# Second buffers for the loads of q and k in an attention and FFN kernel, loads issued a pair earlier, and a new table of times for its scheduler

## The chip, the cores and the metric

One core of a Trainium2 chip runs the whole program. The metric is the time of one execution on the device in microseconds (us). The engines are TensorE (PE; its weight loads are PEld), VectorE (DVE), ScalarE (ACT), GpSimd (POOL) and SyncE (SP), which in this kernel issues every DMA, in order, from one queue.

## The reference

Attention with pairs of queries averaged, then a feed-forward layer whose gate is a cosine. Everything is float32; q and k are drawn eight times larger than v.

```python
# q, k, v: (8 batches, 8 heads, 1152, 64)
q_pool = q.reshape(B, H, S // 2, 2, D).mean(axis=3)          # 576 queries
scores = (1 / sqrt(D)) * matmul(q_pool, k.transpose(0, 1, 3, 2))
scores = scores - max(scores, axis=-1)
attn = exp(scores); attn = attn / (sum(attn, axis=-1) + 1e-09)
x = matmul(attn, v)              # to (8 * 576, 512): heads side by side
h = x @ w_in                     # 512 x 2048
out = (h * cos(h)) @ w_out       # 2048 x 512
```

## The kernel before

**Precision.** Each float32 operand is split in two float16 parts, high and low, and a product is made of two or three float16 matmuls.

**Pairs and units.** The work is cut into 32 pairs (two heads of one batch), pair `n`. A pair has ten units: unit 0 takes the 64 remaining queries of each head, units 1 to 9 take one block of 128 keys each against 512 queries of both heads. A unit makes scores on PE (tile `st`, L880, and L900 for unit 0), the exponential on ACT (`e`, L926), the float16 high part on ACT (`pp`, L929), the low part on POOL or DVE (`pp`, L935 and L931; for unit 0's short rest `pps`), and one unit later the products with v on PE (`ava`, `avb`, L950). The first four pairs (`NDIR`) run the products with v in float32 and without the split (L921).

**What is prepared for a pair ahead of it.** This is what the change touches, step by step:

- k comes in two pieces, J0 (4 of the 9 blocks) and J1 (5). `load_k` loads a piece into `kld` (L576), `prep_k` splits it into `kst` (ACT L604, POOL L605), `transpose_k` transposes it by DMA into one of three `k1` (L650), `copy_k` copies that to one of two `k2` (L657).
- `load_q` loads q into `qld` by four DMAs (two of 256 KB at L586, two of 32 KB at L593). `pool_q` adds the two queries of a pair in place (POOL L611). `prep_q1` writes the high part into `q1s` (L622 on ACT in the first four pairs, then L624 on DVE), and `transpose_q1` transposes that into one of three `q1T` (L629). `prep_q2` writes the low part into `qs2` (POOL L637, L643).
- The row maxima: `mains` and the `mx_` steps multiply q1T with k on PE (`mx`, L675, L693, L715, L732), and DVE reduces each result to maxima (`mxs`, L685, L703, L725, L742), which frees the bank for PE's next one. `m_write` puts the maxima into `qs2`, and `transpose_q2` transposes it into one of two `q2T` (L764).
- `load_v` loads v into its one buffer `vld` (L770), `v_max_begin` reduces its absolute maximum (DVE L777), writes it to DRAM as `row` (512 bytes, L398) and reads it back spread over all partitions as `am` (L400), `v_max_end` reduces that (L405), `prep_v` and `prep_v_lo` split v (ACT L801, DVE L810).

`qld`, `kld`, `kst` and `qs2` have one buffer each, so a load can only be issued when the pair before is done with the tile.

**The FFN** runs beside the attention as a stream of pieces: xT by DMA transposes (L1115), first matmuls (`f`, L1195), evacuation and cosine (L1217 to L1221, L1144, L1150), the split of the gate (`g`, ACT L1159, POOL L1160), second matmuls (L1251) and output (L1267, L1273). The FFN weights are loaded and split during the first pairs. What is left of the FFN after the last pair is the tail.

**What sets the order.** The program is first written down in one order: at each unit of the running pair `p`, the entries `(dp, di, step)` of `JOBS` with `di` equal to the unit run `step(p - dp)`; so `(-2, 1, pool_q)` prepares pair `p + 2` at unit 1 of pair `p`. Then `arrange` lays every engine's instructions anew: it goes through the program in an estimated time, with a cost for each instruction (`estimate`, `transfer`), a delay between engines (`SEM`), and the buffers' limits (`BUFS`); whenever an engine is free it takes, of its instructions whose inputs are ready in that estimate, the one that was written first. The result is fixed in the program: on the chip each engine runs its list in order.

```python
    JOBS = [
        (-2, 0, lambda n: load_k(n, J0)),
        (-2, 0, load_q),
        (-2, 1, lambda n: prep_k(n, J0)),
        (-2, 1, pool_q),
        ...
```

Of the kernel before, what the change touches and what calls it, by code (L numbers as in the profile page):

```python
# [9 lines left out]
F32 = mybir.dt.float32  # L10
# [42 lines left out]
    "e": NE, "pp": NPP, "q1T": 3, "q2T": 2, "xp": NXP, "xT": NXT, "g": NG, "f": 2,  # L53
    "vam": 4, "es": 1, "pps": 1, "amx": 4,
}
POOL_BUFS = {"sb1": 1, "sb2": 2, "psum": 1, "dram": 1}
SIZES = {"float32": 4, "uint32": 4, "int32": 4, "float16": 2}
SEM = 0.10
BOOST = {}
FILL_LATE = 0  # L60
COLD = 0

# [25 lines left out]
def estimate(ins, kind, rd, wr):  # L88


    eng = str(ins.engine).split(".")[-1]
    n = max([a[2] for a in rd + wr] or [1])
    psum = any(str(a[0].space).endswith("PSUM") for a in rd)
    big = sum(a[2] > 1 for a in rd)
    if eng == "PE":
        return max(n_out(wr) * 0.000421, 0.027), False
    if eng == "Pool":
        return 0.08 + 0.00205 * n, True
    if eng == "Activation":
        return 0.19 + 0.0009 * n, False  # L100
    if kind == "InstTensorReduce":
        return 0.1 + 0.00109 * n, False
    if kind == "InstTensorTensor" or (kind == "InstTensorScalarPtr" and big > 1):
        return 0.14 + 0.00112 * n, not psum
# [26 lines left out]
def arrange(tc, nc, extra, fill):  # L131
# [3 lines left out]
    for i in rec:  # L135
        rd, wr = boxes(i)
        eng = str(i.engine).split(".")[-1]
        if eng == "PE":
# [7 lines left out]
            size = tuple(i.tile_size)  # L146
            c = max(n_out(wr) * 0.000421, 0.027)
            if COLD and i.name in fill:
                c = 0.112
            if rd[0][4] == 4:  # L150
                c = max(n_out(wr) * 0.00345, 0.112)
            if size[0] == 64 and tuple(i.tile_position)[0] == 64:
                c = 0.0
            nd["cost"] += c
            nd["tile"] = size[0]
        else:
            nd = dict(eng=eng, ins=[], rd=[], wr=[], cost=0.0, lock=False)
            nodes.append(nd)
            if eng == "SP":
                nd["cost"] = 0.06  # L160
                nd["dma"], nd["lat"] = transfer(type(i).__name__, rd[0], wr[0])
# [156 lines left out]
def tile_attention_ffn(  # L318
# [253 lines left out]
    def load_k(n, js):  # L572
        b, hp = divmod(n, HP)
        nj = js.stop - js.start
        kt = sb1.tile([P, 2, KT - RB, D], F32, tag="kld", name="kld")
        nc.sync.dma_start(  # L576
            kt[:, :, 0:nj],
            k[b, 2 * hp : 2 * hp + 2].rearrange("h (p j) d -> p h j d", p=P)[:, :, js],
        )
        kld[n] = kt[:, :, 0:nj]  # L580

    def load_q(n):
        b, hp = divmod(n, HP)
        qt = sb1.tile([P, NSL, 2, D], F32, tag="qld", name="qld")
        for h in range(2):
# [13 lines left out]
    def prep_k(n, js):  # L599
        kv = kld[n].rearrange("p h j d -> p j h d")  # L600
        nj = js.stop - js.start
        ks = sb1.tile([P, KT - RB, 4, D], F16, tag="kst", name="kst")[:, 0:nj]
        hi = ks[:, :, 0::3, :]
        nc.scalar.copy(hi, kv)  # L604
# [216 lines left out]
    def mains(c, ts):  # L821
# [628 lines left out]
```

## Time and profile before

| what | value |
|---|---|
| median of 3 runs | 1704.35 us (1699.76 to 1707.55) |
| the profiled execution | 1700.43 us, of which the span from first to last instruction is 1698.6 us |
| mean granted TensorE clock | 0.975 of full speed |
| busy share of the span | PE 92%, ACT 72%, DVE 69%, PEld 63%, POOL 53% |
| DMA | 147.36 MB, mean 87 GB/s |

The profile is of one execution. "Idle before <- releaser" says how long an engine stood and what ended it. In a list of waits the three numbers are the total in us, the number of times and the longest. The chain is the work that ended last, followed back from the end. The granted clock is what the throttle allowed TensorE; a busy PE at half clock does half the work.

### The profile page before, as it was taken

What the parts mean: (1) busy time and instruction counts of PE and PEld (TensorE: products, weight loads), DVE (VectorE), ACT (ScalarE), POOL (GpSimd) and SP (SyncE); (2) the same over time, 40 slices, a digit from 0 to 9 for tenths busy, and PEclk for the clock granted to TensorE, in tenths of its full rate; (3) what the DMA queues carried; (4) which work ended last, traced back from release to release, by engine and by line L of the source; (5) the groups of instructions that cost most, each with busy time, mean ns of one, the idle gap of its engine ahead of it and who ended that gap; (6) DMA issues with size and microseconds to landing.
All of it is one profiled execution on the core that took longest, in us unless ns stands there. A gap on an engine that the chain in (4) does not pass through costs nothing.

```text
span 1698.6 us, 40564 instructions
## 1 busy us (share of the span) xinstructions
PE 1570.6 (92%) x17080; PEld 1070.4 (63%) x17080; DVE 1175.2 (69%) x1686; ACT 1217.3 (72%) x1484; POOL 903.5 (53%) x766
## 2 busy tenths in 40 slices
PE   3898999998999988989999999999999999997998
PEld 1677777664766555655766566666666666665664
DVE  5887887678768767777866677787777777632332
ACT  2445468887887877876987686988688878884442
POOL 3323355567575754656575456666746574461222
PEclk9999999999999999999999999999999999998999
DMA  9976745235535453244534324345424442101000
GB/s 197 197 165 130 153 116 75 64 86 109 95 57 114 84 110 63 66 90 95 97 80 96 75 50 101 80 86 105 100 57 97 81 108 60 27 21 27 13 26 19
DMA packets 340662, 147.36 MB, mean 87 GB/s; under 512 B 247808, under 2 KB 323584, under 8 KB 340480
## 3 DMA queue, kind: packets, MB, share of 16 engines
q1 hardware_dynamic: 340480, 144.78, 41.2%
q8 instruction: 133, 2.18, 0.6%
q14 instruction: 49, 0.40, 0.1%
HBM read 76.55 MB, written 10.50 MB: 51 GB/s over the span
## 4 chain that ended last, share of the span: by engine, by line
PE 69%; DVE 10%; DMA 8%; ACT 6%; issue 3%; POOL 3%; SPq 2%; POOLq 0%; ACTq 0%; DVEq 0%
PE f L1251 20%; PE f L1195 16%; PE st L880 11%; PE ava L950 6%; PE avb L950 5%; PE mx L675 5%; DMA qld<-in_q_dram 4%; DVE mxs L685 2%; DVE q1s L624 2%; ACT e L926 2%; PE avb L1019 2%; PE mx L715 1%; DMA k<-kst 1%; POOL pp L935 1%; DMA xT<-xs 1%
## 5 line engine op out<-in xcount | busy, mean ns | idle before, releaser
L935 POOL TENSOR_TENSOR pp<-e,pp 128x512 f16<-128x512 f32 x374 | 453.2, 1234 | 303.9 <-ACT pp L929 155.2
L1195 PE MATMUL f<-xT,w 128*128 128x256 f16 x3456 | 415.0, 276 | 14.7 <-DVE y L1221 8.6
L685 DVE TENSOR_REDUCE mxs<-mx 128x2 f32<-128x1024 f32 x252 | 307.8, 1221 | 148.1 <-PE mx L675 146.9
L926 ACT ACTIVATE e<-st,eb 128x1024 f32<-128x1024 f32 x280 | 311.1, 1111 | 129.4 <-PE st L880 100.4
L1195 PEld LDWEIGHTS <-w 128*128 128x128 f16 x3456 | 340.7, 99 | 88.8 <-issue 17.9
L1251 PE MATMUL f<-w,g 128*128 128x512 f16 x1728 | 396.4, 380 | 0.0
L929 ACT CAST pp<-e 128x1024 f16<-128x1024 f32 x280 | 292.4, 1044 | 7.7
L950 PEld LDWEIGHTS <-pp 128*128 128x128 f16 (+1 forms) x7392 | 247.4, 100 | 69.0 <-POOL pp L935 14.5
L1251 PEld LDWEIGHTS <-g 128*128 128x128 f16 x1728 | 166.9, 98 | 193.0 <-issue 3.8
L1160 POOL TENSOR_TENSOR g<-hsc,g 128x512 f16<-128x512 f32 x144 | 194.3, 1374 | 148.5 <-ACT g L1159 140.9
L950 PE MATMUL ava<-vc,pp 128*128 128x64 f16 (+4 forms) x4784 | 245.1, 200 | 12.3 <-POOL pp L935 9.2
L880 PE MATMUL st<-q1T,k 128*128 128x512 f16 x576 | 224.0, 389 | 11.1 <-ACT e L926 8.5
L880 PE MATMUL st<-q2T,k 128*128 128x512 f16 x576 | 223.5, 388 | 0.0
L950 PE MATMUL avb<-vc,pp 128*128 128x65 f16 (+1 forms) x3312 | 207.2, 202 | 3.1 <-POOL pp L935 3.0
L675 PE MATMUL mx<-k,q1T 128*128 128x512 f16 x504 | 157.3, 395 | 25.3 <-DVE mxs L685 9.4
L1221 DVE SCALAR_TENSOR_TENSOR y<-f,r1a,y 128x512 f32<-128x512 f32 x144 | 107.1, 746 | 95.2 <-ACT y L1220 93.1
L880 PEld LDWEIGHTS <-k 128*128 128x128 f16 x1152 | 103.0, 100 | 101.4 <-issue 21.9
L931 DVE TENSOR_TENSOR pp<-e,pp 128x1024 f16<-128x1024 f32 x93 | 134.0, 1440 | 35.1 <-ACT pp L929 34.0
L1217 ACT ACTIVATE hsc<-f,r 128x512 f32<-128x512 f32 x144 | 98.4, 683 | 80.3 <-PE f L1195 80.1
L1150 DVE TENSOR_TENSOR hsc<-hsc,y 128x512 f32<-128x512 f32 x144 | 129.6, 950 | 36.6 <-ACT y L1144 36.2
L605 POOL TENSOR_TENSOR kst<-kld,kst 128x512 f16<-128x512 f32 x64 | 88.9, 1389 | 98.3 <-ACT kst L604 83.7
L675 PEld LDWEIGHTS <-q1T 128*128 128x128 f16 x512 | 47.9, 102 | 92.9 <-issue 36.0
(118 smaller groups left out, 1717.6 us busy)
## 6 DMA issues: line engine op xcount, KB each, us to landing
vld<-in_v_dram SPq DMA_DIRECT2D x32, 576.0 KB, 4.3
qld<-in_q_dram SPq DMA_DIRECT2D x64, 256.0 KB, 4.4
kld<-in_k_dram SPq DMA_DIRECT2D x32, 320.0 KB, 3.8
kld<-in_k_dram SPq DMA_DIRECT2D x32, 256.0 KB, 3.2
wraw<-in_moe_w_in_dram SPq DMA_DIRECT2D x8, 1024.0 KB
wraw<-in_moe_w_out_dram SPq DMA_DIRECT2D x8, 1024.0 KB, 6.0
out_dram<-ob SPq DMA_DIRECT2D x32, 256.0 KB, 2.7
k<-k SPq DMA_DIRECT2D x64, 80.0 KB, 3.1
```

What stands on the lines that cost most here:

```text
L675: nc.tensor.matmul(m[:, h, :], q1T[n][:, 2 * t + h, :], k1[n % 3][:, c * RB : (c + 1) * RB, h, :], start=True, stop=True, skip_group_check ...
L685: nc.vector.reduce_max(mxs[n][:, 2 * t : 2 * t + 2, c], m, axis=AX.X)
L880: nc.tensor.matmul(s[:, h, :].rearrange("p (t c) -> p t c", c=P), w[:, j, h, :], x[:, h : 2 * QT : 2, :], start=part == 0, stop=part == 1, ...
L926: nc.scalar.activation(e, s, AF.Exp, scale=exp_scale, bias=eb)
L929: nc.scalar.copy(pp[:, 0], e)
L931: nc.vector.tensor_sub(pp[:, 1], e, pp[:, 0])
L935: nc.gpsimd.tensor_sub(pp[:, 1, c], e[:, c], pp[:, 0, c])
L950: mm = nc.tensor.matmul(out, w, x, start=start, stop=False, skip_group_check=True)
L1150: nc.vector.tensor_mul(hj, hj, y[:, j : j + 2])
L1160: nc.gpsimd.tensor_sub(gt[:, 1], hj, gt[:, 0])
L1195: mm = nc.tensor.matmul(ps[:, fi, :], w1[wt][:, hp, fs], ck.xT[hp][:, xi, cs], start=n == 0, stop=n == 3 * HP - 1, skip_group_check=True,)
L1251: nc.tensor.matmul(po, gt[:, gi, f % 2, ts_], w2[wt][:, f, :], start=f == 0 and (gi, wt) == (0, 0), stop=f == NF - 1 and (gi, wt) == (1, 0),)
```

## The change

1. `qld`, `kld` and `kst` get two buffers each, and there are two `qs2` (by the parity of the pair); the dictionaries of k pieces are keyed by pair and piece.
2. The loads of k and q move from the unit of their use in pair `p` for `p + 2` to units 5, 6 and 9 for `p + 3`. At the start, three pairs' loads are written ahead of the first unit instead of two.
3. `load_v` moves from unit 8 for `p + 2` to unit 0 for `p + 1`, the steps after it by one unit.
4. The table of times: the delay between engines becomes 0.21 after PE, 0.08 after ACT and 0.06 after the others, instead of 0.10 for all; an issue on SP costs 0.55 (a transpose 1.35) instead of 0.06; POOL, ACT, DVE and PE costs are set anew, and a half-width matmul counts half.

```diff
 BUFS = {
     "e": NE, "pp": NPP, "q1T": 3, "q2T": 2, "xp": NXP, "xT": NXT, "g": NG, "f": 2,
-    "vam": 4, "es": 1, "pps": 1, "amx": 4,
+    "vam": 4, "qld": 2, "kld": 2, "kst": 2, "es": 1, "pps": 1, "amx": 4,
 }
-SEM = 0.10
+HAND = {"PE": 0.21, "Activation": 0.08}
...
     if eng == "Pool":
-        return 0.08 + 0.00205 * n, True
+        return 0.16 + 0.00206 * n, True
     if eng == "Activation":
-        return 0.19 + 0.0009 * n, False
+        return 0.21 + 0.00088 * n, False
...
-            c = max(n_out(wr) * 0.000421, 0.027)
+            c = max(n_out(wr) * 0.0004167 + 0.0025, 0.0295)
...
-                nd["cost"] = 0.06
+                nd["cost"] = 1.35 if "Transpose" in type(i).__name__ else 0.55
...
-        fin = end + SEM
+        fin = end + HAND.get(e, 0.06)
...
-    qs2 = fix.tile([P, NSL, P], F16, name="qs2")
-    nc.gpsimd.memset(qs2, 0.0)
+    qs2s = [fix.tile([P, NSL, P], F16, name=f"qs2_{i}") for i in range(2)]
+    for t in qs2s:
+        nc.gpsimd.memset(t, 0.0)
...
-        kt = sb1.tile([P, 2, KT - RB, D], F32, tag="kld", name="kld")
+        kt = sb1.tile([P, 2, KT - RB, D], F32, tag="kld", bufs=2, name="kld")
...
-        qt = sb1.tile([P, NSL, 2, D], F32, tag="qld", name="qld")
+        qt = sb1.tile([P, NSL, 2, D], F32, tag="qld", bufs=2, name="qld")
...
-        ks = sb1.tile([P, KT - RB, 4, D], F16, tag="kst", name="kst")[:, 0:nj]
+        ks = sb1.tile([P, KT - RB, 4, D], F16, tag="kst", bufs=2, name="kst")[:, 0:nj]
...
     JOBS = [
-        (-2, 0, lambda n: load_k(n, J0)),
-        (-2, 0, load_q),
+        (-3, 5, lambda n: load_k(n, J0)),
+        (-3, 6, load_q),
+        (-3, 9, lambda n: load_k(n, J1)),
         (-2, 1, lambda n: prep_k(n, J0)),
         (-2, 1, pool_q),
         (-2, 1, lambda n: transpose_k(n, J0)),
-        (-2, 2, lambda n: load_k(n, J1)),
         (-2, 2, prep_q1),
...
-        (-2, 8, load_v),
...
-        (-1, 0, v_max_begin),
+        (-1, 0, load_v),
+        (-1, 1, v_max_begin),
...
-        (-1, 4, v_max_end),
-        (-1, 5, prep_v),
-        (-1, 6, lambda n: prep_v_lo(n, (0,))),
-        (-1, 7, lambda n: prep_v_lo(n, (1,))),
+        (-1, 5, v_max_end),
+        (-1, 6, prep_v),
+        (-1, 7, lambda n: prep_v_lo(n, (0,))),
+        (-1, 8, lambda n: prep_v_lo(n, (1,))),
...
-    for n in (0, 1):
+    for n in (0, 1, 2):
```

How the instructions move, for pair 12 as the example. In the rows below a name carries its buffer's number, and the changed kernel's line numbers are mostly one or two off. SP before, from v's load of pair 11 to pair 12's transpose of q1 (`qld_6576` is pair 12's q, `kst_6669` and `kld_6767` its k):

```order
L770 DMA vld_6417<-in_v_dram 128x2x576
L657 DMA k2_1_70<-k1_2_107 64x5x128 x2
L398 DMA row_6589<-mxa_6587 128x1
L586 DMA qld_6576<-in_q_dram 128x4x128
L593 DMA qld_6576<-in_q_dram 64x128 x2
L650 DMA_TRANSPOSE k1_0_105<-kst_6669 128x8x128
L576 DMA kld_6767<-in_k_dram 128x2x320
L586 DMA qld_6576<-in_q_dram 128x4x128
L400 DMA am_6591<-row_6589 128x128
L1073 DMA left_95<-lx_6648 64x64 x2
L629 DMA_TRANSPOSE q1T_6772<-q1s_73 128x10x128
```

The load of q stands right behind `row`, and three rows ahead of the transpose that needs it. SP of the changed kernel, at the load of pair 12's q (`qld_6280`):

```order
L627 DMA_TRANSPOSE q1T_5241<-q1s_75 128x10x128
L396 DMA row_5162<-mxa_5160 128x1
L649 DMA_TRANSPOSE k1_1_108<-kst_5296 128x10x128
L584 DMA qld_6280<-in_q_dram 128x4x128
L591 DMA qld_6280<-in_q_dram 64x128
L1074 DMA left_97<-lx_5136 64x64
L574 DMA kld_6214<-in_k_dram 128x2x256
L591 DMA qld_6280<-in_q_dram 64x128
L584 DMA qld_6280<-in_q_dram 128x4x128
```

It now stands just behind pair 10's transpose of q1 (`q1T_5241`). And 24 rows further on, SP of the changed kernel at pair 12's transpose of q1, from v's load of pair 11 (`vld_6589`):

```order
L771 DMA vld_6589<-in_v_dram 128x2x576
L656 DMA k2_1_70<-k1_2_109 64x5x128 x2
L627 DMA_TRANSPOSE q1T_6774<-q1s_75 128x10x128
L649 DMA_TRANSPOSE k1_0_107<-kst_6842 128x10x128
L396 DMA row_6674<-mxa_6672 128x1
L584 DMA qld_7779<-in_q_dram 128x4x128
L591 DMA qld_7779<-in_q_dram 64x128 x2
L574 DMA kld_7722<-in_k_dram 128x2x256
L584 DMA qld_7779<-in_q_dram 128x4x128
```

The transposes of pair 12 now stand ahead of `row`, and what stands behind `row` are loads for later pairs. POOL before, from pair 12's split of k to its split of q (`pps_6563` is pair 10's):

```order
L605 TENSOR_TENSOR kst_6669<-kld_6574,kst_6669 128x4x128
L935 TENSOR_TENSOR pp_6470<-e_6468,pp_6470 128x512 x2
L935 TENSOR_TENSOR pp_6557<-e_6555,pp_6557 128x512 x2
L935 TENSOR_TENSOR pps_6563<-es_6561,pps_6563 128x128
L611 TENSOR_TENSOR qld_6576<-qld_6576 128x9x64
L935 TENSOR_TENSOR pp_6758<-e_6756,pp_6758 128x512 x2
L605 TENSOR_TENSOR kst_6840<-kld_6767,kst_6840 128x5x128
L935 TENSOR_TENSOR pp_6831<-e_6829,pp_6831 128x512 x2
```

The pooling of q (L611) stands behind pair 10's `pps`, and the `pp` of pair 10 stand behind it. POOL of the changed kernel at the same step of pair 12 (`kst_6667`, `qld_6280`; `pps_5823` is pair 9's, and pair 8's stands six rows ahead of the first row shown):

```order
L603 TENSOR_TENSOR kst_6667<-kld_6214,kst_6667 128x4x128
L609 TENSOR_TENSOR qld_6280<-qld_6280 128x9x64
L636 TENSOR_TENSOR qs2_1_72<-qld_5433,q1s_75 128x4x2x64
L936 TENSOR_TENSOR pp_5554<-e_5552,pp_5554 128x512 x2
L642 TENSOR_TENSOR qs2_1_72<-qld_5433,q1s_75 64x64
L936 TENSOR_TENSOR pp_5628<-e_5626,pp_5628 128x512 x2
L642 TENSOR_TENSOR qs2_1_72<-qld_5433,q1s_75 64x64
L609 TENSOR_TENSOR qld_7036<-qld_7036 128x9x64
L936 TENSOR_TENSOR pp_5817<-e_5815,pp_5817 128x512 x2
L936 TENSOR_TENSOR pps_5823<-es_5821,pps_5823 128x128
```

The pooling of pair 12's q has moved ahead of pair 9's `pps`, and that of pair 13 (`qld_7036`) follows it within the same pair.

More of the change, by code (lines that the diff above doesn't have):

```diff
@@ L57 @@
 SIZES = {"float32": 4, "uint32": 4, "int32": 4, "float16": 2}
-SEM = 0.10
+HAND = {"PE": 0.21, "Activation": 0.08}
 BOOST = {}
 FILL_LATE = 0
-COLD = 0
 def boxes(ins):
@@ L103, in estimate @@
     if kind == "InstTensorTensor" or (kind == "InstTensorScalarPtr" and big > 1):
-        return 0.14 + 0.00112 * n, not psum
+        return 0.15 + 0.00106 * n, not psum
     if kind == "InstTensorScalarPtr":
@@ L146, in arrange @@
             size = tuple(i.tile_size)
-            c = max(n_out(wr) * 0.000421, 0.027)
-            if COLD and i.name in fill:
-                c = 0.112
+            c = max(n_out(wr) * 0.0004167 + 0.0025, 0.0295)
             if rd[0][4] == 4:
-                c = max(n_out(wr) * 0.00345, 0.112)
-            if size[0] == 64 and tuple(i.tile_position)[0] == 64:
-                c = 0.0
+                c = 2 * max(n_out(wr) * 0.00167 + 0.0025, 0.112)
+            if size[1] == 64:
+                c *= 0.5
             nd["cost"] += c
-            nd["tile"] = size[0]
+            nd["tile"] = size
         else:
@@ L249, in arrange @@
     table = None
-    mode = 128
+    mode = (128, 128)
     order = {e: [] for e in engines}
@@ L280, in arrange @@
         if e == "PE" and nd["tile"] != mode:
-            c += 0.1
+            c += 0.15
             mode = nd["tile"]
@@ L579, in load_k @@
         )
-        kld[n] = kt[:, :, 0:nj]
+        kld[n, js.start] = kt[:, :, 0:nj]
     def load_q(n):
         b, hp = divmod(n, HP)
-        qt = sb1.tile([P, NSL, 2, D], F32, tag="qld", name="qld")
+        qt = sb1.tile([P, NSL, 2, D], F32, tag="qld", bufs=2, name="qld")
         for h in range(2):
@@ L599, in prep_k @@
     def prep_k(n, js):
-        kv = kld[n].rearrange("p h j d -> p j h d")
+        kv = kld.pop((n, js.start)).rearrange("p h j d -> p j h d")
         nj = js.stop - js.start
-        ks = sb1.tile([P, KT - RB, 4, D], F16, tag="kst", name="kst")[:, 0:nj]
+        ks = sb1.tile([P, KT - RB, 4, D], F16, tag="kst", bufs=2, name="kst")[:, 0:nj]
         hi = ks[:, :, 0::3, :]
@@ L605, in prep_k @@
         nc.gpsimd.tensor_sub(ks[:, :, 1:3, :], kv, hi)
-        kst[n] = ks
+        kst[n, js.start] = ks
     def pool_q(n):
@@ L634, in prep_q2 @@
     def prep_q2(n):
+        qs2 = qs2s[n % 2]
         qs = qld.pop(n)
@@ L651, in transpose_k @@
             k1[n % 3][:, js].rearrange("p j h c -> p (j h) c"),
-            kst.pop(n).rearrange("p j a d -> p (j a d)"),
+            kst.pop((n, js.start)).rearrange("p j a d -> p (j a d)"),
         )
@@ L744, in m_write @@
     def m_write(n):
+        qs2 = qs2s[n % 2]
         m = sb2.tile([P, NSL], F32, tag="m", name="m")
@@ L762, in transpose_q2 @@
     def transpose_q2(n):
+        qs2 = qs2s[n % 2]
         t = sb1.tile([P, NSL, P], F16, tag="q2T", bufs=2, name="q2T")
```

## The prediction

> **What bounds the kernel now.** I read the page first (engines, then the chain that ended last), then busy time by stretches, then one stall in order of time.
>
> ```profile
> span 1698.6 us, 40564 instructions
> PE 1570.6 (92%) x17080; PEld 1070.4 (63%) x17080; DVE 1175.2 (69%) x1686; ACT 1217.3 (72%) x1484; POOL 903.5 (53%) x766
> ...
> PE 69%; DVE 10%; DMA 8%; ACT 6%; issue 3%; POOL 3%; SPq 2%; POOLq 0%; ACTq 0%; DVEq 0%
> PE f L1251 20%; PE f L1195 16%; PE st L880 11%; PE ava L950 6%; PE avb L950 5%; PE mx L675 5%; DMA qld<-in_q_dram 4%; DVE mxs L685 2%; DVE q1s L624 2%; ACT e L926 2%; PE avb L1019 2%; PE mx L715 1%; DMA k<-kst 1%; POOL pp L935 1%; DMA xT<-xs 1%
> ```
>
> TensorE sets the time: busy for 92% of the span, and 69% of the chain. The largest single thing in the chain that is not TensorE's own work is the load of q, 4% of 1698.6 = 68 us. Where is TensorE idle?
>
> ```profile
> 0.00:265.00 265.00, 213.15 (x1804) 161.43 (x1805) 204.30 (x332) 126.07 (x150) 100.43 (x83) 0.95 0.78 159
> 265.00:1540.00 1275.00, 1214.81 (x14356) 816.47 (x14354) 919.07 (x1285) 1030.63 (x1248) 769.97 (x658) 0.98 0.39 80
> 1540.00:1698.60 158.60, 142.60 (x928) 92.54 (x924) 51.86 (x70) 60.60 (x87) 33.08 (x26) 0.94 0.08 21
> ```
>
> Columns: stretch and length, then busy time of PE, PEld, DVE, ACT, POOL, then granted clock, DMA share, GB/s. The start (weights arriving, DMA share 0.78) holds 265 − 213.15 = 51.9 us of PE idle time, the middle 1275 − 1214.81 = 60.2 us, the tail of pure FFN 16.0 us. No other engine is near full in the middle (ACT 81%), so what can be won there is those 60.2 us and what the clock of 0.98 takes. One of the middle's stalls, rows picked in order of time (start, length, ..., [idle before <- what ended it]):
>
> ```profile
> 500.35 0.33 SPq L398 DMA_DIRECT2D row<-mxa  x1
> 504.73 0.61 SPq L586 DMA_DIRECT2D qld<-in_q_dram  x1
> 515.81 1.41 POOL L611 TENSOR_TENSOR qld<-qld 128x576 f32<-128x576 f32 x1 [7.36 <-DMA qld<-in_q_dram]
> 517.25 4.08 DVE L624 CAST q1s<-qld 128x1024 f16<-128x1024 f32 x3 [3.11 <-POOL qld L611]
> 521.57 1.22 DVE L703 TENSOR_REDUCE mxs<-mx 128x8 f32<-128x1024 f32 x1
> 522.84 1.39 PE L715 MATMUL mx<-k,q1T 128*128 128x512 f16 x4 [3.67 <-DVE mxs L703]
> ```
>
> The q load issued at 504.73 lets POOL go only at 515.81, 11 us later. POOL stood 7.36 us at the pooling of q with ready work behind it, DVE then stood at the cast of it, a reduce that would have freed a bank for PE stood behind the cast, and PE lost 3.67 us. The load was not big but badly placed: it was issued 4.4 us after the tiny write `row`, and these are the median landings:
>
> ```profile
> vld<-in_v_dram SPq DMA_DIRECT2D x32, 576.0 KB, 4.3
> qld<-in_q_dram SPq DMA_DIRECT2D x64, 256.0 KB, 4.4
> ...
> am<-row SPq DMA_DIRECT2D x32, 64.0 KB, 3.0
> ...
> row<-mxa SPq DMA_DIRECT2D x32, 0.5 KB, 7.7
> ```
>
> `row` takes 7.7 us although it is 0.5 KB, and this load behind it took 11 instead of 4.4. In sum over the run:
>
> ```profile
> POOL qld L611 <- DMA qld<-in_q_dram: 78.8, 15, 14.2
> ...
> ACT kst L604 <- DMA kld<-in_k_dram: 30.7, 10, 11.3
> ...
> POOL qs L637 <- DMA q2T<-qs: 19.9, 9, 5.9
> ...
> ACT kst L604 <- DMA k<-kst: 13.0, 7, 3.4
> ```
>
> **Part 1, the loads (the term that counts).** The middle has eight PE gaps of about 3 us or more. I followed each back in order of time: seven end at a late q load, one (at 598) at a late k load. Their stretches (first, last, sum of the eight), and then the 10 us behind each of them:
>
> ```profile
> 419.80:425.10 5.30, 0.35 (x6) 0.23 (x6) 2.71 (x2) 0.79 (x2) 4.16 (x4) 0.93 0.48 119
> ...
> 1227.20:1230.20 3.00, 0.08 (x3) 0.07 (x2) 2.90 (x4) 0.12 (x1) 3.00 (x4) 0.95 0.05 10
> sum 36.00, PE 1.09 PEld 0.62 DVE 25.96 ACT 8.99 POOL 20.71; mean PE 0.14 PEld 0.08 DVE 3.24 ACT 1.12 POOL 2.59
> ```
>
> ```profile
> 425.10:435.10 10.00, 8.47 (x101) 5.37 (x102) 8.87 (x15) 6.70 (x8) 7.89 (x7) 0.87 0.74 155
> 522.90:532.90 10.00, 10.00 (x82) 5.49 (x82) 9.75 (x22) 5.63 (x8) 2.61 (x3) 0.83 0.64 130
> 604.10:614.10 10.00, 9.10 (x142) 5.30 (x142) 7.47 (x9) 8.52 (x10) 6.90 (x7) 0.77 0.28 55
> 651.80:661.80 10.00, 9.45 (x72) 6.58 (x73) 7.61 (x17) 6.93 (x12) 2.12 (x3) 0.77 0.14 43
> 748.10:758.10 10.00, 10.00 (x62) 4.64 (x62) 4.98 (x15) 8.26 (x11) 4.51 (x5) 0.80 0.31 74
> 796.60:806.60 10.00, 9.71 (x138) 5.64 (x138) 9.46 (x18) 7.75 (x10) 6.55 (x6) 0.84 0.42 57
> 931.10:941.10 10.00, 10.00 (x59) 4.54 (x59) 5.17 (x14) 8.64 (x11) 2.99 (x4) 0.74 0.39 95
> 1230.20:1240.20 10.00, 10.00 (x105) 6.91 (x105) 6.12 (x12) 7.26 (x11) 2.73 (x4) 0.84 0.33 74
> ```
>
> Idle: 36.00 − 1.09 = 34.9 us. Clock: PE looks busy behind each gap, but at a granted clock of 0.74 to 0.87. The lost share is 0.13 + 0.17 + 0.23 + 0.23 + 0.20 + 0.16 + 0.26 + 0.16 = 1.54 times 10 us = 15.4 us. Together 50.3 us, 6.3 us a stall.
>
> The Trainium skill, "Perfetto Trace Analysis", section "Identifying the Most-Contended Engine", says that matmul busy time is a poor measure of headroom, because matmuls are pipelined. By busy time alone this term would be 34.9 us and the time about 15 us higher than below; by the page the slow-clock stretches have to be counted although they read as busy, and the rows at 522.90 and 931.10 (PE 10.00 of 10.00, clock 0.83 and 0.74) side with the page.
>
> Do the loads really come early? The order says so (rows in the section on the change): the second q load of that pair stood three rows ahead of its q1T transpose on SP, now 26 rows; POOL's pooling of q for pair 12 stood right behind pair 10's pps, now it stands between those of pairs 8 and 9. That is one to two pairs earlier. A pair is ten units, and the row of the 280 wide exponentials gives a unit:
>
> ```profile
> L926 ACT ACTIVATE e<-st,eb x280: 1090/1113/1135, 233.9 to 1537.2; 128x1024 f32<-128x1024 f32 x140
> ```
>
> (1537.2 − 233.9)/279 = 4.67 us. A load that lands even 11 us after issue is then hidden behind more than 47 us of other work. The same DMAs are issued (four for q, two for k a pair, about 0.6 us of SP each, as at 504.73); they now stand ahead of the transposes and v's work of earlier pairs, which costs those a few such issues, against slacks of units.
>
> What is late next: q1T has three buffers, so its transpose now waits for the scores of the pair three before to end. Its first reader comes four units, 18.7 us, later. No stall by itself.
>
> **Part 2, second kst and qs2.** They end the waits of 13.0 us (ACT) and 19.9 us (POOL) above. Neither ended one of the eight gaps, and both engines have room (81% and 60% busy in the middle), so I count 0; ends 0 and −4 us (the 32.9 us times POOL's and ACT's 9% of the chain, rounded up). The extra memset runs on POOL before data arrive: 0.
>
> **Part 3, the start.** Pair 2's loads join the first ones. Ahead of pair 0's second q load now stand pair 0's second k load (320 KB) and pair 1's two small ones (64 KB).
>
> ```profile
> 21.33 1.03 PE L675 MATMUL st<-k,q1T 128*128 128x512 f16 x2 [21.33 <-DMA q1T<-q1s]
> ...
> 96.52 1.40 POOL L611 TENSOR_TENSOR qld<-qld 128x576 f32<-128x576 f32 x1 [14.20 <-DMA qld<-in_q_dram]
> 97.50:100.40 2.90, 0.06 (x1) 0.00 (x0) 0.37 (x1) 2.40 (x6) 2.66 (x3) 0.95 0.62 175
> 100.40:110.40 10.00, 9.27 (x70) 5.68 (x70) 7.62 (x13) 4.38 (x6) 3.42 (x2) 0.67 0.64 141
> ```
>
> At the start's 159 GB/s, 384 KB are 2.5 us, and three more issues 1.8 us: a loss of 2 to 4 us on the first matmul. In return the stall at 97.5 goes: 2.8 us idle and 3.3 us of clock. Ends +4 and −6; I take −3.
>
> **Part 4, v's work a unit or two later, and the table.**
>
> ```profile
> L777 DVE TENSOR_REDUCE mxa<-vld 128x1 f32<-128x1152 f32 x32 | 43.0, 1344 | 5.4 <-DMA vld<-in_v_dram 5.4
> ```
>
> ```profile
> SPq L770 <- DVE vc L810: 54.8, 18, 9.7
> ```
>
> Between load_v and v_max_end stand five units instead of six, 23.4 us. The chain in it is 4.3 us load, 1.3 us reduce, 7.7 us row, 3.0 us am: 16.3 us. It fits: 0. The table sets every engine's order anew. Its effect no row shows. A gain is bounded by the middle's idle time outside the eight gaps, 60.2 − 34.9 = 25 us; for a loss I take the same size, four stalls of 6.3 us. I take 0, the middle.
>
> **Sum.** The profiled execution took 1700.4 us (span 1698.6). 1700.4 − 50.3 − 3 = 1647. The median of the three runs, 1704.35, is 3.9 above that execution; I add it: 1651, and say 1650. Likeliest range 1632 to 1668: part 2's −4 and some 14 us of the table's either way.
>
> **Rivals.**
> 1. *Half of it comes back as another wait.* SP is one queue in order. At a pair's boundary it now holds two k2 copies, q1T and the second k transpose in a row, and whatever is issued behind `row` lands late. If half the stalls return: 1650 + 25 = 1675. For it: `row` is unchanged at 7.7 us. Against: in the rows of the order q1T stands ahead of `row`, loads behind it. Chance 0.15.
> 2. *The table helps too*, taking more than 18 of the 25 us: below 1632, about 1620. For it: SP's cost was 0.06 in the old table where a q load's issue takes 0.61. Against: the remaining idle pieces are small and many. Chance 0.10.
> 3. *Slower: v's chain.* Its slack falls from 28.0 (six units) − 16.3 = 11.7 us to 7.1 us. If SP issues vld, row or am over 7 us late in all, DVE stands at the reduce of vld or of am with PE's reduces behind it, the same stall as now at q1s, 6.3 us each. Eight such stalls eat the gain; from ten of the 28 pairs on the kernel is over 0.5% slower; in every second pair it would be 1650 + 14 × 6.3 = 1738. For it: SP is in order and v's load waits there for its one buffer (54.8 us in 18 waits, up to 9.7). Against: DVE waited only 5.4 us in all for vld before. Chance 0.07.
> 4. *The moved steps hold up POOL and DVE.* The pooling ran while both stood idle; now it runs beside DVE's two-input operations.
>
> ```profile
> L611 POOL TENSOR_TENSOR qld<-qld x32: 1395/1403/2401, 9.5 to 1403.3; 128x576 f32<-128x576 f32 x32
> ```
>
> It takes 1.40 us alone and up to 2.40 in company. If in each of 28 pairs one of the two stands for its 1.40 us and all of it is on the path, that is 39 us: 1689. Against: DVE and POOL make 13% of the chain, which leaves 5 us. The Trainium skill, "SBUF — State Buffer", section "Who interferes with whom", says that VectorE and GpSimd share a port pair by an exclusive lock, and that the loser stands for the whole instruction; the 2.40 agrees that one of them stands, and nothing here shows for how many pairs. Chance 0.03.
> 5. *It does not do what it says*: the loads, issued early, get stuck on SP and arrive as before: 1700. Against: 26 rows of distance. Chance 0.05.
>
> **Chances.** 0.60 for the likeliest, and 0.15, 0.10, 0.07, 0.03, 0.05 for the rivals in turn. About 0.5%, 8.5 us, is what a measurement of this kernel tells from no change. Faster by more: 0.60 + 0.15 + 0.10 + 0.03 = 0.88; within: 0.05; slower: 0.07. The range from 1622 to 1686 takes in rival 1 with its spread and most of rival 2.
>
> **What would show it.** Right: POOL's wait for qld falls from 78.8 us to under 10, ACT's for kld from 30.7 to under 5; the middle's PE idle time falls from 60 us to about 25, with a granted clock of 0.99 to 1.00; `row` is still near 7.7 us. Part 3 is right if the first matmul starts 2 to 4 us after 21.3 us and no stall stands near 97. Wrong: a new line among the longest waits in which DVE or POOL stand for a transpose or for vld or am, or PE gaps of 3 us at pair boundaries.

## The result, and the profile after

| | median us | range | runs |
|---|---|---|---|
| before | 1704.74 | 1699.76 to 1707.55 | 4 |
| after | 1684.64 | 1679.24 to 1686.29 | 4 |

The ratio is 0.988, with a 95% interval of 0.9848 to 0.9912: about 20 us faster, where 54 were forecast. The profiled execution after is the fastest one, 1679.24 us. Its page, first the span and the engines, then the chain:

```profile
span 1677.5 us, 40539 instructions
PE 1557.0 (93%) x17080; PEld 1063.4 (63%) x17080; DVE 1187.6 (71%) x1686; ACT 1216.8 (73%) x1484; POOL 911.6 (54%) x767
...
PE 68%; DVE 11%; DMA 8%; ACT 6%; SPq 3%; issue 3%; POOL 1%; ACTq 0%; POOLq 0%; DVEq 0%
PE f L1252 21%; PE f L1196 17%; PE st L881 11%; PE ava L951 6%; PE avb L951 5%; PE mx L674 5%; DVE mxs L684 2%; DMA row<-mxa 2%; ACT e L927 2%; DMA am<-row 2%; SPq L627 2%; PE mx L714 1%; DMA k<-kst 1%; PE st L901 1%; PE avb L1020 1%
```

The load of q, 4% of the chain before, has left it. But DMA still holds 8%: `row` and `am`, 2% each, stand in its place, and SP's issue of q1's transpose (L627) adds 2% under SPq. Busy time by stretches (columns as in the prediction):

```profile
0.00:265.00 265.00, 210.39 (x1886) 161.15 (x1887) 224.51 (x341) 132.95 (x158) 106.20 (x93) 0.97 0.76 166
265.00:1530.00 1265.00, 1210.73 (x14315) 814.50 (x14314) 914.02 (x1284) 1025.21 (x1243) 774.07 (x651) 0.99 0.40 79
1530.00:1677.00 147.00, 135.90 (x884) 87.78 (x881) 49.11 (x61) 58.59 (x84) 31.31 (x24) 0.97 0.07 20
```

The middle keeps 1265 − 1210.73 = 54.3 us of PE idle time; about 25 were forecast. The waits:

```profile
POOL qld L609 <- DMA qld<-in_q_dram: 67.6, 11, 17.9
...
PE st L674 <- DMA q1T<-q1s: 25.5, 1, 25.5
ACT kst L602 <- DMA k<-kst: 23.2, 11, 5.3
DVE q1s L622 <- DMA q1T<-q1s: 22.8, 10, 5.3
POOL qs L636 <- DMA q2T<-qs: 22.4, 7, 7.6
ACT kst L602 <- DMA kld<-in_k_dram: 19.4, 5, 7.4
DVE amx L403 <- DMA am<-row: 19.2, 8, 5.4
```

The fourth and the last line are new in size: before, DVE did not wait at q1s for a transpose, and for `am` 5.4 us in all. Gone is DVE's wait at q1s for POOL (34.4 us in ten), the one that had reached PE. POOL still waits for q loads (50.2 us of the 67.6 lie in the middle, where it was 41.6 before), but no longer with DVE standing behind it.

One new stall in order of time (start, length, ..., [idle before <- what ended it]):

```profile
320.32 0.33 SPq L396 DMA_DIRECT2D row<-mxa  x1
...
324.16 7.78 SPq L627 DMA_TRANSPOSE q1T<-q1s  x1
...
331.99 2.30 SPq L649 DMA_TRANSPOSE k<-kst  x1
...
335.48 0.69 DVE L622 CAST q1s<-qld 128x1024 f16<-128x1024 f32 x1 [3.14 <-DMA q1T<-q1s]
335.63 0.53 SPq L398 DMA_DIRECT2D am<-row  x1
336.09 1.22 DVE L702 TENSOR_REDUCE mxs<-mx 128x8 f32<-128x1024 f32 x1
```

The transpose of q1, issued 3.8 us after `row`, holds SP for 7.78 us (1.3 us is the median of this trace's 176 transposes). DVE stands at the cast for the next pair, which needs the one `q1s` that this transpose still reads; the reduce behind it is late, and PE loses 3.8 us from 334.43 on. The other new kind:

```profile
496.27 0.66 SPq L396 DMA_DIRECT2D row<-mxa  x1
505.81 0.33 SPq L398 DMA_DIRECT2D am<-row  x1
511.87 0.28 DVE L403 TENSOR_REDUCE amx<-am 128x1 f32<-128x128 f32 x1 [4.28 <-DMA am<-row]
...
517.42 1.21 DVE L702 TENSOR_REDUCE mxs<-mx 128x8 f32<-128x1024 f32 x1
518.68 1.27 PE L714 MATMUL mx<-k,q1T 128*128 128x512 f16 x4 [4.04 <-DVE mxs L702]
```

From `row` to the reduce of `am` it took 15.6 us here, where I had put 10.7 (7.7 and 3.0).

**Accounts of the middle.** There are nine new gaps of 1.5 us and more. By the rows ahead of each, five follow this wait at `q1s`, three the wait for `am`; the ninth, at 595, was not traced back. Here are the first, the last and the sum, and then the 10 us behind seven of them, by their clock (first and last two):

```profile
334.43:338.23 3.80, 0.00 (x2) 0.00 (x0) 1.83 (x2) 1.76 (x3) 0.99 (x1) 1.00 0.79 194
...
1211.15:1213.56 2.41, 0.00 (x0) 0.00 (x0) 2.35 (x5) 1.76 (x3) 0.77 (x1) 1.00 0.47 133
sum 24.22, PE 0.03 PEld 0.01 DVE 20.15 ACT 12.43 POOL 15.16; mean PE 0.00 PEld 0.00 DVE 2.24 ACT 1.38 POOL 1.68
```

```profile
338.23:348.23 10.00, 10.00 (x95) 6.39 (x95) 8.15 (x21) 8.54 (x13) 3.75 (x4) 0.83 0.32 76
...
1032.38:1042.38 10.00, 10.00 (x119) 7.16 (x119) 8.98 (x20) 7.45 (x10) 3.41 (x2) 0.71 0.13 37
1213.56:1223.56 10.00, 10.00 (x154) 7.92 (x154) 7.76 (x20) 9.92 (x11) 4.26 (x4) 1.00 0.14 38
```

Five of the seven clocks are 0.83, one 0.71, one 1.00, and 1.00 behind the other two gaps: 5 × 1.7 + 2.9 = 11.4 us. So the eight stalls (50.3 us) went, new ones of 24.2 + 11.4 = 35.6 us came, and idle pieces too small to follow grew from 25.3 to 54.3 − 24.2 = 30.1 us. That leaves 50.3 − 35.6 − 4.8 = 9.9 us. The exponentials say the same:

```profile
L927 ACT ACTIVATE e<-st,eb x280: 1089/1114/1133, 221.5 to 1515.2; 128x1024 f32<-128x1024 f32 x140
```

From the first to the last wide one it is 1293.7 us, before 1303.3: 9.6 less. The start gained 233.9 − 221.5 = 12.4, the tail lost 0.9; together the 21.1 us between the two spans.

### The profile page after: what moved, and what is told of

Its sections match the earlier page's. It is cut to its first block, busy times and chain, and to the rows that moved or that the text cites. A ratio compares the mean times of both kernels' runs of the same rounds, so it can differ in the third digit from the quotient of the medians.

```text
span 1677.5 us, 40539 instructions
## 1 busy us (share of the span) xinstructions
PE 1557.0 (93%) x17080; PEld 1063.4 (63%) x17080; DVE 1187.6 (71%) x1686; ACT 1216.8 (73%) x1484; POOL 911.6 (54%) x767
## 4 chain that ended last, share of the span: by engine, by line
PE 68%; DVE 11%; DMA 8%; ACT 6%; SPq 3%; issue 3%; POOL 1%; ACTq 0%; POOLq 0%; DVEq 0%
PE f L1252 21%; PE f L1196 17%; PE st L881 11%; PE ava L951 6%; PE avb L951 5%; PE mx L674 5%; DVE mxs L684 2%; DMA row<-mxa 2%; ACT e L927 2%; DMA am<-row 2%; SPq L627 2%; PE mx L714 1%; DMA k<-kst 1%; PE st L901 1%; PE avb L1020 1%
## 5 line engine op out<-in xcount | busy, mean ns | idle before, releaser
L936 POOL TENSOR_TENSOR pp<-e,pp 128x512 f16<-128x512 f32 x374 | 457.9, 1246 | 342.2 <-ACT pp L930 186.6
L951 PE MATMUL avb<-vc,pp 128*128 128x65 f16 (+1 forms) x3312 | 203.8, 200 | 1.7 <-POOL pp L936 1.6
L674 PE MATMUL mx<-k,q1T 128*128 128x512 f16 x504 | 153.2, 386 | 22.0 <-DVE mxs L684 15.3
L1151 DVE TENSOR_TENSOR hsc<-hsc,y 128x512 f32<-128x512 f32 x144 | 137.5, 1003 | 38.7 <-ACT y L1145 38.5
L932 DVE TENSOR_TENSOR pp<-e,pp 128x1024 f16<-128x1024 f32 x93 | 135.5, 1457 | 41.3 <-ACT pp L930 41.2
```

The source lines that it names most:

```text
L674: nc.tensor.matmul(m[:, h, :], q1T[n][:, 2 * t + h, :], k1[n % 3][:, c * RB : (c + 1) * RB, h, :], start=True, stop=True, skip_group_check ...
L932: nc.vector.tensor_sub(pp[:, 1], e, pp[:, 0])
L936: nc.gpsimd.tensor_sub(pp[:, 1, c], e[:, c], pp[:, 0, c])
L951: mm = nc.tensor.matmul(out, w, x, start=start, stop=False, skip_group_check=True)
L1151: nc.vector.tensor_mul(hj, hj, y[:, j : j + 2])
```

## The experiments

Ratios are to the kernel before, run on the same chip in the same stretch of time. "Middle" is the time from the first to the last of the 280 wide exponentials in the profiled execution.

| run | what | ratio | 95% | first | middle |
|---|---|---|---|---|---|
| before | | 1 | | 233.9 | 1303.3 |
| after | the change | 0.9880 | 0.9848 to 0.9912 | 221.5 | 1293.7 |
| E1 | change, old table | 1.0087 | 1.0054 to 1.0121 | 251.5 | 1309.2 |
| E2 | new table alone | 1.0114 | 1.0081 to 1.0146 | 241.1 | 1317.5 |
| E3 | change, order moved a little | 0.9934 | 0.9913 to 0.9954 | 233.4 | 1292.6 |
| E4 | change, two q1s | 0.9895 | 0.9867 to 0.9923 | 231.0 | 1287.8 |
| E5* | before, row on ACT's queue | 0.9971 | 0.9955 to 0.9988 | 232.0 | 1324.2 |
| E6* | change, row on ACT's queue | 0.9970 | 0.9949 to 0.9992 | 233.6 | 1324.3 |
| E7* | change, old table, two q1s | 1.0169 | 1.0144 to 1.0193 | 245.0 | 1338.8 |
| E8* | change, v's load earlier | 0.9864 | 0.9839 to 0.9889 | 232.5 | 1310.0 |
| E9 | before without row | 0.9641 | 0.9619 to 0.9664 | 222.0 | 1256.7 |
| E10 | change without row | 0.9611 | 0.9592 to 0.9631 | 216.3 | 1254.3 |
| E11 | change without row, two q1s | 0.9583 | 0.9563 to 0.9604 | 211.7 | 1252.5 |
| E12 | change without row, old table | 0.9699 | 0.9676 to 0.9722 | 232.2 | 1254.0 |
| E13 | E9 and row written for nobody | 0.9932 | 0.9907 to 0.9957 | 241.5 | 1278.2 |
| E14 | the same, 64 bytes each | 0.9632 | 0.9599 to 0.9665 | 219.2 | 1254.7 |
| E15 | the same, 4 bytes, 512 apart | 0.9627 | 0.9595 to 0.9660 | 218.7 | 1255.0 |
| E16 | the same, into SBUF | 0.9619 | 0.9583 to 0.9655 | 216.8 | 1254.7 |

\* These four ran where the kernel before took 1723 us instead of about 1700. Only their ratios compare with the others, and the changed kernel as it stands was not run beside them.

### The parts of the change: E1, E2, E3

E1 takes the changed kernel and puts the old table back:

```diff
-HAND = {"PE": 0.21, "Activation": 0.08}
+SEM = 0.10
 # estimate, transfer's callers and arrange as in the kernel before; BUFS, JOBS and the buffers as changed
```

> The changed kernel with its buffers, loads and step times kept, and the scheduler's table of times put back to the old one. Theory A (the forecast gain came, and half of it was given back by new DVE waits at the single q1s buffer and at the late am): the table does little, the time stays within 8 us of 1685, and the lines DVE q1s <- DMA q1T<-q1s and DVE amx <- DMA am<-row stay at 15 us or more together. Theory B (the loads alone give the forecast 50 us and the new table's order costs 30 of them): 1655 or below.

Measured: 1715.24 us, ratio 1.0087. Neither theory: the early loads with the old order are slower than no change at all. The wait at the single q1s is there, and larger:

```profile
DVE q1s L625 <- DMA q1T<-q1s: 58.6, 17, 8.1
```

E2 is the reverse, the new table in the kernel before.

> The kernel before with the new table of times alone. Theory A: within 8 us of 1704, with POOL's waits for the q load still near 79 us, for nothing in it makes the loads come sooner. Theory B: slower than before by 20 to 30 us, 1725 to 1735. A third, that the table gave the whole gain: 1685.

Measured: 1719.22 us, ratio 1.0114. Each half of the change alone loses about 1%, and the two together win 1.2%. Its profile has the old stall: q loads issued 2.4 and 0.6 us after `row` (at 601.31 and 797.37 us) let POOL go only 9.6 and 9.8 us later. So the parts don't add, and the question became what they have in common.

E3 asks what mere reordering does:

```diff
-        kt = sb1.tile([P, 2, KT - RB, D], F32, tag="kld", bufs=2, name="kld")
+        kt = sb1.tile([P, 2, nj, D], F32, tag=f"kld{js.start}", name="kld")
```

> The changed kernel with the two buffers of the k load given names of their own, one for the first and one for the second part (each part used the same one of the two before as well). No buffer is won or lost; only the order moves a little where the scheduler breaks ties otherwise. Theory A: 1685 within 4 us. Theory C (any new order moves the time by several us, and the result of 20 us is the forecast plus such chance): over 6 us away from 1685 on either side.

Measured: 1688.17 us, ratio 0.9934; its interval lies just above that of the change. By the ratios a new order with the same resources is worth half a per cent (the medians themselves, taken at different times, are 3.5 us apart, within theory A's 4). In the two profiled executions all of it is in the start (first wide exponential at 233.4 instead of 221.5); the middles agree (1292.6 and 1293.7). So the 12.4 us that the start gained in the profile after are not to be put down to the loads, which come as early in E3.

### The two new waits, one by one: E4, E7, E8

E4 gives q1s a second buffer, on top of E3:

```diff
-    q1s = fix.tile([P, NSL + 1, 2, D], F16, name="q1s")
-    nc.gpsimd.memset(q1s[:, 2 * QT :], 0.0)
+    q1ss = [fix.tile([P, NSL + 1, 2, D], F16, name=f"q1s_{i}") for i in range(2)]
+    for t in q1ss:
+        nc.gpsimd.memset(t[:, 2 * QT :], 0.0)
 # prep_q1, transpose_q1 and prep_q2 use q1ss[n % 2]
```

> As the run with the k load's buffers named apart, and a second q1s buffer, so that the cast of the next pair's q no longer waits for the transpose of the last one. Theory A: the line DVE q1s <- DMA q1T<-q1s (22.8 us, ten waits) goes under 5 us; of the nine new PE gaps of 1.6 us and more the five that end there go, about 15 us idle and 4 half-clock stretches of 3.4 us (1.7 us each): 1685 - 15 to 22 = 1663 to 1670. Theories B and C: no more than 6 us from the run without the second q1s; also if the transpose itself is late, since the waits then move to the scores' matmuls or to the transposes.

Measured: 1682.70 us, ratio 0.9895, 5.5 us less than E3. The wait shrank as told, the stalls only in part: the middle has five PE gaps of 1.5 us and more with 14.9 us in all, where E3 has eight of about that size with 22.4.

```profile
DVE amx L404 <- DMA am<-row: 22.6, 9, 5.9
...
DVE q1s L624 <- DMA q1T<-q1s: 5.1, 2, 3.2
```

```profile
329.96 0.33 SPq L397 DMA_DIRECT2D row<-mxa  x1
...
333.81 7.73 SPq L630 DMA_TRANSPOSE q1T<-q1s  x1
...
345.14 0.69 DVE L624 CAST q1s<-qld 128x1024 f16<-128x1024 f32 x1 [3.17 <-DMA q1T<-q1s]
```

It is the same stall as in the change (there at 320 to 335): SP stands 7.73 us at the transpose behind `row`. The single q1s was where much of the delay surfaced, not where it came from.

> The changed kernel with the old table of times (1715 us, q1s waits of 58.6 us in 17) and a second q1s buffer. Theory A: the waits at the one q1s are what the loads alone lose by; they go under 10 us and the time comes down to 1685 to 1698. Rival: the order that the old table sets is the loss, whatever the buffers: 1707 or more.

Measured: ratio 1.0169, not faster than E1 without the second buffer (1.0087, measured where the kernel before took 1701). DVE's wait at q1s for a transpose is still 47.2 us in nine, where theory A had under 10; the longest, 9.5 us, follows a transpose that held SP for 8.9 us, issued 3 us behind `row`. So a second q1s did not make up the loss of the early loads. Since the wait did not go, the run alone does not rule theory A out; E12 below, the same table with a single q1s and without `row`, does.

E8 gives v's chain its slack back:

```diff
+        (-2, 8, load_v),
...
-        (-1, 0, load_v),
-        (-1, 1, v_max_begin),
+        (-1, 0, v_max_begin),
```

> The changed kernel with v's load put back to its old step (two units earlier than now) and its first max reduction one unit earlier, the end of v's chain where it is: seven units of slack instead of five. Theory A: the line DVE amx <- DMA am<-row falls from 19.2 us to under 8, the three gaps of 1.8, 4.0 and 2.9 us that end there go with their slow clock: 10 to 14 us less, 1671 to 1676. Rival F (am is late because SP is held behind row, wherever the chain starts): same within 6 us, am's wait over 12 us.

Measured: ratio 0.9864, within the interval of the change, about 3 us better where 10 to 14 were expected. The wait for `am` fell to 12.2 us, not below 8, as rival F had it. Slack was not the main point either: `am` is still late when v comes two units earlier.

### Row on another queue: E5, E6

```diff
-        nc.sync.dma_start(row.rearrange("a p -> p a"), mx)
+        nc.scalar.dma_start(row.rearrange("a p -> p a"), mx)
 # arrange gives a DMA of ACT the latency that it gave SP's
```

> The kernel before, with the tiny write row issued by ACT on its own queue instead of SP's; the scheduler is told of it, all else stays. Theory D (the stalls hang on row: whatever stands within some 8 us behind it on SP's queue is held until it has landed, the q load before the change, the q1T transpose after it): the q loads land in about 4 us wherever they stand, most of the eight stalls go, 1650 to 1670. Rival E (row holds the transfers of all queues, or the q loads are late for the load of the transfers at that place): the waits for the q load stay near 79 us and the time within 8 us of 1702.

Measured: ratio 0.9971. The waits stay:

```profile
POOL qld L612 <- DMA qld<-in_q_dram: 100.0, 18, 11.5
```

One of them in order of time; `row` is now on ACTq:

```profile
627.52 0.62 SPq L587 DMA_DIRECT2D qld<-in_q_dram  x1
628.20 1.25 SPq L594 DMA_DIRECT2D qld<-in_q_dram  x2
629.50 0.60 SPq L587 DMA_DIRECT2D qld<-in_q_dram  x1
629.67 0.34 ACTq L399 DMA_DIRECT2D row<-mxa  x1
632.67 5.81 SPq L658 DMA_DIRECT2D k<-k  x2
638.54 1.45 SPq L651 DMA_TRANSPOSE k<-kst  x1
638.98 1.40 POOL L612 TENSOR_TENSOR qld<-qld 128x576 f32<-128x576 f32 x1 [11.49 <-DMA qld<-in_q_dram]
```

The q load was issued ahead of `row`, on another queue, and still took until 638.98. The transfers of this stretch, ahead of `row`'s packets (627.0 to 630.5) and behind them (632.5 to 638.5), both with q's load outstanding:

```profile
DMA packets 860, 0.54 MB, mean 153 GB/s; under 512 B 47, under 2 KB 860, under 8 KB 860
...
DMA packets 458, 0.17 MB, mean 28 GB/s; under 512 B 317, under 2 KB 456, under 8 KB 456
...
q1 hardware_dynamic: 456, 0.15, 18.4%
q8 instruction: 1, 0.02, 5.8%
```

From 153 GB/s to 28, with DMA engines mostly idle; a single 16 KB fetch of instructions took 5.8% of 16 × 6 us = 5.6 us (the median of this run's fetches of 8 and 16 KB in the middle is 1.0 us). This is not a queue waiting its turn: for some 7 us every transfer in sight crawls, the instruction fetch with them. Counted over all rows of the changed kernel's middle (packets of 256 to 1024 bytes), 106 KB moved in the us before `row`'s packets, 22 to 43 KB in each of the seven us from there on, and over 100 again nine us after. Part of that fall is only that less is asked for then: in E15 below, where a like write costs nothing, the same count is 114 KB and then 36 to 69.

The Trainium skill, "DMA: Bandwidth & Descriptors", section "Issuing engines are not separate DMA queues", says that DMAs of all issuing engines run on the same 16 DMA engines and that spreading them saves only issue time. This run agrees: 100.0 us of waits against 78.8.

> The changed kernel with row on ACT's queue in the same way. Theory D: no transpose of q1 holds SP for over 4 us (seven did for 3.4 to 7.8 us), the line DVE q1s <- DMA q1T<-q1s falls from 22.8 us to under 8, and with it five of the nine new gaps: 1660 to 1672. Rival E: the transposes behind row still hold SP for 5 to 8 us, 1680 to 1690.

Measured: ratio 0.9970. The wait at q1s is 38.6 us (22.8 in the change), and SP still stands at transposes for up to 6.8 us in the middle. Theory D falls, rival E stands. That its ratio is 0.9% above that of the change is not explained beyond that; the change itself was not run beside it.

### Row taken away: E9 to E12

v's maximum over the partitions is now made by PE, with the partition maxima rounded to f16; only the power of two at or below the maximum is used for v's scale.

```diff
-        vam[n] = all_max_begin(mxa, "vam")
+        vam[n] = mxa                     # f16 now
...
+    def v_max_mid(n):                    # two units later
+        am = psum.tile([P, 2, 512], F32, tag="mx", name="vmx")
+        nc.tensor.matmul(am[:, 0, 0:P], vam[n].broadcast_to([P, P]), id16, ...)
+        vam[n] = all_max_of(am[:, 0, 0:P])
```

> The kernel before, with v's maximum over the partitions taken by one 128x128 matmul against an identity in f16 (as the weights' maxima are) instead of the write row and the read am: both DMAs are gone, PE gets 32 short matmuls more, DVE reduces the same 128 values from PSUM. Theory E (row holds up the transfers of every queue for some 9 us; the eight stalls are that hold): the q load lands early wherever it stands, POOL's waits for it in the middle fall to under 20 us, most of the forecast's 50 us come here: ratio to before 0.970 to 0.982. If instead the loads are late for want of a second buffer, as the change's words say: ratio 0.995 to 1.003.

Measured: 1636.72 us, ratio 0.9641: 63 us from a kernel whose loads still have one buffer and are issued as late as before. Span, engines, and the two waits:

```profile
span 1639.6 us, 40480 instructions
PE 1556.6 (95%) x17112; PEld 1066.7 (65%) x17112; DVE 1178.8 (72%) x1686; ACT 1217.2 (74%) x1484; POOL 910.5 (56%) x767
```

```profile
POOL qld L614 <- DMA qld<-in_q_dram: 41.2, 14, 6.1
...
ACT kst L607 <- DMA kld<-in_k_dram: 10.6, 3, 7.5
```

Between 265 us and the last wide exponential its trace has only two PE gaps over 1.4 us (2.0 and 1.9). The waits for q that are left (24.1 us in the middle, a little over the 20 expected) stop no matmul for long.

> The changed kernel without row and am in the same way. Theory E: the new stalls (q1T's transpose held on SP, am late) are the same hold met at another place; they go, and the granted clock in the middle reaches 0.99 to 1.00: ratio to before 0.965 to 0.978, and within 6 us of the kernel before without row, since nothing is left for the early loads to hide. Theory A alone (one q1s buffer, whatever row does): the line DVE q1s <- DMA q1T<-q1s stays over 15 us and the ratio at 0.982 to 0.990.

Measured: 1633.32 us, ratio 0.9611. The clock in the middle is 1.00 and the wait at q1s has gone with `row` (1.7 us), with one q1s buffer as before. The intervals of E9 and E10 overlap: with `row` away, the whole change is worth 3 us or nothing.

> The changed kernel without row and am and with two q1s buffers (the k load's two buffers named apart to make room). Theory E: within 5 us of the run without row alone. Theory A: 8 us or more faster than that.

Measured: 1627.33 us (1626.81 to 1630.07), the fastest version, 72 us below the kernel before on that chip (1699.45). It is 6 us below E10, most of it in the start; theory E had said within 5.

> The changed kernel's buffers, loads and steps with the old table of times, without row and am. With row this was 0.9% slower than before. Theory E (the early loads lost there because the transposes fell into row's hold): the loss goes, ratio 0.968 to 0.985. Theory C (the order that the old table sets is bad by itself): 1.000 or more.

Measured: ratio 0.9699. E1's loss of 0.9% has become a gain of 3%. The middle is that of E10 (1254.0 and 1254.3); what the old table still costs, 16 us, is in the start.

Put together: without `row`, four orders and buffer sets have middles of 1252.5 to 1256.7 us, 4 us apart. With `row`, the first six rows of the table (all from chips of one speed) lie between 1287.8 and 1317.5, 30 us apart. So in the middle the order matters mainly because it decides what falls into the stretch behind `row`; the start still differs by 20 us without it (211.7 to 232.2).

### What in row does it: E13 to E16

Each writes `row` again beside the matmul, at the same place in the program, read by nobody:

```diff
+        mxw = sb2.tile([P, 16], F32, tag="mxw", name="mxw")
+        nc.vector.tensor_copy(mxw, mxa.broadcast_to([P, 16]))
+        row = dram.tile([P, 1], F32, tag="vam", bufs=4, name="row")     # E13
+        nc.sync.dma_start(row, mxw[:, 0:1])
...
 # E14: row of [P, 16], all of mxw.  E15: row of [P, P], its column 0.  E16: row of [P, 1] in SBUF.
```

> The kernel before without row and am as above, and row written again where it was, 128 times 4 bytes side by side in DRAM, read by nobody (two tiny DVE copies come with it, under 0.5 us a pair). Theory E1 (the write itself holds the transfers): the waits for the q load come back over 60 us and the ratio to before goes to 0.985 or more, against 0.964 without it. E2 (the chain through am was the cost): within 0.005 of 0.964.

Measured: 1689.02 us, ratio 0.9932: 0.029 of the 0.036 that E9 had won are lost again to 512 bytes a pair that nobody reads. The waits follow:

```profile
POOL qld L614 <- DMA qld<-in_q_dram: 66.9, 16, 14.6
ACT kst L607 <- DMA kld<-in_k_dram: 21.5, 7, 11.0
```

The rest, 0.007, is that of the chain through `am` or of a different order; that wasn't taken apart.

> The same with 64 bytes of each partition written, 8 KB side by side in DRAM. If the hold comes from elements under 64 bytes: 0.964 to 0.970. If it comes from 128 separate small writes of any size: as the run with 4 bytes.

Measured: 0.9632, no hold.

> The same with 4 bytes of each partition, 512 bytes apart in DRAM. If the hold comes from many writes into one small piece of DRAM: 0.964 to 0.970. If from 4-byte writes to DRAM wherever they lie: as the run with 4 bytes side by side.

Measured: 0.9627, no hold, though the elements have 4 bytes as in E13. The wait for q is back near E9's 41.2 us:

```profile
POOL qld L614 <- DMA qld<-in_q_dram: 37.3, 16, 6.0
```

> The same with 4 bytes of each partition written into SBUF, each to its own partition. If the hold is DRAM's: 0.964 to 0.970. If it is that of 128 4-byte elements in the DMA engines: as the run with 4 bytes side by side.

Measured: 0.9619, no hold.

In E13, E15 and E16 every engine has the same instructions in the same order (E14 differs in some ten places on DVE and PE), so a different order is no rival here. From issue to landing `row` takes 1.8, 1.8 and 1.9 us (medians of E14, E15, E16), where it took 7.7 in the kernel before.

So the cause is shown: 128 writes of 4 bytes side by side in one 512-byte piece of DRAM. Bigger elements, the same elements further apart, or the same elements to SBUF cost nothing that this kernel shows. The Trainium skill, "DMA: Bandwidth & Descriptors", section "Specifications", says that below 512 bytes a DMA engine does a read-modify-write. Size alone does not make the hold: the elements of E14 (64 bytes) and E15 (4 bytes) are under 512 too. That many read-modify-writes of one place wait for each other would fit; no run shows it. Nor does a run show from which distance on, between 4 and 64 bytes, the hold ends.

## Why the prediction was wrong, step by step

- **Part 1, the early loads: right that they hide the eight stalls, wrong on the cause and on the next wait.** The eight stalls went, and with E9's middle, 46.6 us shorter than before, their price of 50.3 us was about right (in part by luck, for E9 takes away more than the late loads). The step that failed is its last one, "What is late next: ... No stall by itself". I looked for the next wait in buffers and counted slack in units, and took `row` for a slow transfer that delays the loads behind it. It delays transfers of every kind: SP at the transposes, `am`, the k copies. Taking the loads out of its way put transposes of q1 there (in the middle, five that held SP for 3.8 to 7.8 us); SP, in order, then held the rest. 35.6 us of stalls came back where I had 0.
- **Part 4, v's chain, "It fits: 0".** The terms came from medians over the run (row 7.7, am 3.0); the stall shown took 15.6 us instead of 10.7, and such waits came to 19.2 us in eight. Rival 3 had the place. E8, with two units more slack, still has 12.2 us of them, so slack, its point of decision, was not the main thing that ran out.
- **Part 4, the table, 0 ± 25.** Alone it costs 18 us, with the early loads it gains 35 (E1 against the change, 0.021 of 1701), and without `row` 15 (E12 against E10), all of it in the start. The middle value of 0 was wrong, and the bound of 25, taken from the middle's small gaps, too small for a table that also decides what meets `row`.
- **Part 3, the start.** The first matmul came 25.5 − 21.3 = 4.2 us later (2 to 4 forecast). The 12.4 us gained by the fourth pair's end are not the loads' (E3 has 0.5): more than half of the 21.1 us between the two profiles is luck of the order. The stall near 97 became one of 1.8 us near 100.
- **Part 2, second kst and qs2.** No run takes them alone, so the 0 is neither borne out nor refuted. But the waits did not end: 13.0 became 23.2 us for kst and 19.9 became 22.4 for qs2. The transposes that they wait for stand on SP.
- **Rival 1** (half comes back as another wait, SP in order at the pair's boundary, loads late behind `row`, 0.15, 1675) is the nearest to what happened. Its price was too low: in the middle four fifths came back, 40.7 of 50.3 us. Its argument against itself, that q1T stands ahead of `row`, was one place of the order taken for all.
- **The signs.** DVE standing for a transpose or for am, named as the sign of a wrong forecast, is what the profile shows. "POOL's wait for qld under 10 us" was the wrong one: it stayed at 67.6 us while the eight stalls went, since what hurt was DVE behind it. ACT's wait for kld (19.4 us, under 5 told) and the middle's PE idle time (54.3, 25 told) missed too; the clock of 0.99 came as told.

## What to carry to other kernels

When stalls share a cause that is a transfer, look at what else moves in that stretch, on all queues and in instruction fetches, before hiding the one victim that stands there: here, moving it only chose the next one. Here the sign was in the rows before: a write of 512 bytes that takes 7.7 us, and a load behind it 11 instead of 4.4. And when a schedule's parts each lose alone and win together, test for a shared disturbance rather than tune the order; with it gone, the orders tried here are 4 us apart in the middle.

## What the runs showed of the hardware

- 128 writes of 4 bytes into 512 contiguous bytes of DRAM slow the transfers of other queues too: in the stall shown from E5, from 153 to 28 GB/s for some 7 us, SP's loads and the instruction fetch alike, with the write on ACT's queue. 32 of them cost this kernel about 50 us (E13 against E14 and E15; by the ratios also against E9). With 64 bytes each, 512 bytes apart, or into SBUF they cost nothing.
- Five transposes of q1 in the change's middle, issued 3.4 to 7.4 us behind such a write, held SP for 3.8 to 7.8 us, where 1.3 us is usual; four others, three of them 0.6 to 2.5 us behind it and one 7.2, took 1.4.
- The slow clock does not follow from the length of one PE gap: in the change it was 0.83 or 0.71 over the 10 us behind gaps of 1.63 us and of 2.88 us and more, and 1.00 behind gaps of 1.59, 1.78 and 2.41 us. The trace shows what sets them apart. Its stretches of half clock all begin on one grid with steps of 3.41 us; in the middle each of them follows a step in which PE stood idle for 1.75 us or more in all, and no step with 1.59 us or less is followed by one. The gap of 1.63 us lies within one step (594.42 to 597.83 us, PE busy for 1.66 of 3.41 us; the clock of the next step is 0.50), while the gap of 2.41 us falls on two (busy for 2.33 and 2.08 of 3.41 us; the clock stays at 1.00). The bound is less sharp in other traces: half clock follows 1.57 us of idle time in E12 and does not follow 1.96 us in E4.
